# A chunked recurrent attention with a gated MLP on one core: filler matmuls, mask program, transfers and down-product waits changed together

## The chip, the core and the metric

One core of a Trainium2 chip runs the kernel as one program on five engines: TensorE (PE, with its weight loads PEld), VectorE (DVE), ScalarE (ACT), GpSimd (POOL) and SyncE (SP, which here only issues DMAs). The metric is the device time of one execution in microseconds; lower is better.

## The reference

The input x has 2048 rows of 640. After a layer norm, attention runs over 64 segments of 32 rows, one after the other: each segment is headed by 8 memory rows, which are the first 8 output rows of the segment before. 32 heads of 128, a causal mask, and the output product Wo. Then a gated MLP with 1728 hidden columns. Both have a residual.

```python
for s in range(n_seg):
    h = jnp.concatenate([mem, xs], axis=1)          # 8 + 32 rows
    q, k, v = h @ Wq, h @ Wk, h @ Wv                 # per head
    p = softmax(where(mask, q k^T * scale, -1e9))
    o = (p v) @ Wo
    mem = o[:, :M]
    outs.append(o[:, M:])
h = x + attention
h2 = h + (relu(gate) * up) @ W_down                  # gate, up: layernorm(h) @ W_gate, W_up
```

The segments form a serial chain; the MLP (rows in four blocks of 512) can only start on rows that are done.

## The kernel before, in words

The program is recorded as a list of operations, each with keys that it reads and writes (`add`, L38). `solve` (L45) turns the keys into semaphore waits; each engine then runs its own operations in the order in which they were recorded. So the order in the source is the order on each engine, and a wait holds up all that is queued behind it on the same engine. A key that names a finer part of a tile gives a wait for that part alone.

**Opening** (masks from L293, the rest L719 to L940). SP issues the 15 weight transfers of W (five row chunks of 1 MB each for K, Q and V), then 8 pieces of Wo (640 KB each, keys ("Wo", half, group)), then one input load. Meanwhile POOL builds constants, among them the two masks `mca` and `mbd` by chains of affine_select (L293 to L316). PE projects K, Q and V for the first segment and the first group of memory-side rows, in the order in which the W chunks land: K and Q chunk by chunk, then `first_values` (L766) for V, chunks 0 to 2, the scores of segment 0 (`scores`, L475), and V chunks 3 and 4. Then come the memory part of the softmax (`pv_mem`, L528), the products with the first half of Wo (`wo_pairs`, L591, four groups, each waits for its Wo piece), the second half (`wo_pass`, L574, four groups), and between them projections and `keep_busy` (L882): matmuls whose result in bank T1 nobody reads. keep_busy(n, cut) issues 4n products of 512 columns, each cut into `cut` matmuls. The segment's result goes through DVE (L614, L615) into act_r, from which segment 1 starts.

**Segments 1 to 63** (from L945). Each projects K, Q and V, does scores, softmax and products with V and Wo, and hands 8 rows on by `fold_split` (L600) and `to_act_split` (L612). `fold_split(bk, eng)` puts its addition (L606) on the engine that it is given. Values are also copied by DMA into VM (`merge_v`, L648), which `pv_x` (L663) reads in the next segment. Every fourth segment projects rows for the four segments to come from act_e (`extra_units`, L789). In segment 60 POOL copies rows into act_e (L1087).

**MLP.** W's space is reused once the projections are done. `load_piece(key)` (L780) takes the next piece of W_gate or W_up off a list (column groups 0 to 255, 256 to 511, 512 to 1023, and so on; from 512 on each group comes in two row halves) and issues it once `key` has been written. xn2T, the normed rows of block 0, is loaded in segment 62 (L996). `gate_up(b, j)` (L839) makes hidden columns 128j to 128j+127; the ones of block 0 begin amid segment 63. `load_down` (L1155) loads W_down in pieces of three row chunks, keys ("Wd", 0) to ("Wd", 6); `down_part` and `down_tails` (L1091, L1106) multiply with it.

In the trace, helpers appear under one line: L386 and L359 are projection matmuls (L359 reuses loaded weights, also in L1100's products), L410 the copies on ACT, L324 all DMA issues, L347 DMA transposes, L121 a wait of its own.

## Time and profile before

| | us |
|---|---|
| median of 3 runs | 1005.47 (1005.17 to 1006.03) |
| the profiled execution | 1004.47 |
| its span, first to last instruction | 1002.7 |
| PE busy | 970.9 (97%), 26,097 matmuls |
| PE weight loads | 537.8 (54%), 24,920 |
| DVE busy | 715.6 (71%) |
| ACT busy | 524.9 (52%) |
| POOL busy | 167.8 (17%) |
| mean granted TensorE clock | 0.997 |

The page's first part gives busy time by engine, the second the span in 40 slices, the fourth the chain of work that ended last: followed back from the last instruction, at each step to what released it. What lies on that chain sets the time; an engine that is idle beside it costs nothing. The span is divided into the opening (0 to 58 us), 63 segments of about 12 us (58 to 821 us), and the MLP, whose first products begin at 813 us. The list of waits adds up, for each line, how long its engine stood idle before it and what ended that. The timeline gives single instructions, and a query by windows the busy time, clock and DMA share of any stretch.

### The profile page before, as it was taken

How to read it: one execution, taken by the hardware profiler on the slowest of the kernel's cores; microseconds unless marked ns; L12 is line 12 of the kernel's file. 1: busy time of each engine (PE TensorE's matmuls, PEld its weight loads, DVE VectorE, ACT ScalarE, POOL GpSimd, SP SyncE). 2: the span in 40 equal slices, each digit the busy share in tenths (PEclk: the TensorE clock that was granted, in tenths of full speed). 3: DMA queues.
4: the chain of work that ended last, by engine and by line, in shares of the span. 5: the costliest groups of instructions: out<-in, count | busy, mean ns of one | idle time of the engine just before them, and what ended most of it. 6: DMA issues, size and time to landing. Idle time of an engine off the chain costs nothing.

```text
span 1002.7 us, 56369 instructions
## 1 busy us (share of the span) xinstructions
PE 970.9 (97%) x26097; PEld 537.8 (54%) x24920; DVE 715.6 (71%) x1863; ACT 524.9 (52%) x1330; POOL 167.8 (17%) x416
## 2 busy tenths in 40 slices
PE   3789999999999999999999999999999999999998
PEld 1255555556555555555556555655555554344443
DVE  2558787878888887888788878787878756345332
ACT  0456666666666666666666666566666643122121
POOL 7011202021302130222022212111110010000000
PEclk9899999999999999999999999999999999999999
DMA  9921212121222122111312131211121168413100
GB/s 374 417 96 36 53 29 53 28 56 55 54 41 54 48 54 46 48 54 47 53 41 63 48 55 40 41 41 39 40 40 34 44 175 242 103 20 93 27 14 26
DMA packets 73103, 73.34 MB, mean 73 GB/s; under 512 B 42304, under 2 KB 59680, under 8 KB 70944
## 3 DMA queue, kind: packets, MB, share of 16 engines
q1 hardware_dynamic: 70736, 68.44, 24.5%
q8 instruction: 200, 3.28, 1.4%
q10 hardware_dynamic: 2128, 1.31, 0.5%
q14 instruction: 39, 0.32, 0.1%
HBM read 37.04 MB, written 6.55 MB: 43 GB/s over the span
## 4 chain that ended last, share of the span: by engine, by line
PE 93%; DMA 3%; SPq 2%; DVE 1%; issue 1%; ACT 0%; POOL 0%; DVEq 0%; ACTq 0%
PE ps L386 47%; PE ps L850 10%; PE ps L359 7%; PE ps L574 7%; PE ps L591 7%; PE ps L634 4%; PE ps L1100 3%; DMA W<-in_A_Wv_dram 3%; PE ps L475 2%; PE ps L663 2%; PE ps L528 2%; SPq L324 1%; DMA Wd<-in_B_W_down_dram 0%; PE ps L889 0%; PE ps L863 0%
## 5 line engine op out<-in xcount | busy, mean ns | idle before, releaser
L386 PE MATMUL ps<-W,act_r 128*32 128x512 bf16 (+1 forms) x8369 | 454.4, 358 | 2.9 <-DVE act_r L615 1.8
L386 PEld LDWEIGHTS ps<-W,act_r 128*32 128x32 bf16 x8369 | 212.9, 96 | 168.3 <-DVE act_r L615 33.1
L410 ACT ACTIVATE tok<-ps 128x512 bf16<-128x512 f32 x190 | 109.4, 594 | 57.1 <-PE ps L386 48.7
L386 PE MATMUL ps<-W,act_e 128*32 128x512 bf16 x1224 | 120.8, 385 | 8.2 <-DMA W<-in_A_Wv_dram 4.2
L405 DVE STREAM_TRANSPOSE Ko<-tox 128x512 bf16<-128x512 bf16 x128 | 89.8, 702 | 38.9 <-ACT tox L410 36.6
L483 POOL COPY Qo<-Qe 128x256 bf16<-128x256 bf16 x64 | 28.0, 437 | 529.4 <-DVE oT L548 522.4
L410 ACT ACTIVATE tox<-ps 128x512 bf16<-128x512 f32 x134 | 79.6, 598 | 53.1 <-PE ps L386 32.0
L554 DVE STREAM_TRANSPOSE oT<-tox 128x512 bf16<-128x512 bf16 x128 | 94.2, 736 | 0.0
L405 DVE STREAM_TRANSPOSE Qo<-tok 128x512 bf16<-128x512 bf16 x124 | 85.5, 690 | 0.8
L359 PE MATMUL ps<-W,act_e 128*32 128x512 bf16 x856 | 85.5, 387 | 0.0
L574 PE MATMUL ps<-Wo,oT 128*32 128x160 bf16 x4032 | 82.4, 233 | 0.9 <-issue 0.9
L591 PE MATMUL ps<-Wo,oT 128*32 128x320 bf16 x2016 | 80.4, 300 | 0.0
L574 PEld LDWEIGHTS ps<-Wo,oT 128*32 128x32 bf16 x4032 | 71.4, 97 | 9.7 <-DVE oT L548 3.1
L410 ACT ACTIVATE Vp<-ps 128x512 bf16<-128x512 f32 x127 | 75.2, 592 | 0.7 <-ACT Vp L410 0.5
L878 ACT ACTIVATE g<-ps 128x512 bf16<-128x512 f32 x52 | 30.1, 593 | 80.1 <-PE ps L850 80.1
L604 ACT ACTIVATE SA<-TA 64x40 f32<-64x40 f32 x126 | 29.5, 234 | 75.8 <-DVE TA L602 75.0
L879 DVE TENSOR_TENSOR hT<-g,ps 128x512 bf16<-128x512 bf16 x52 | 35.7, 687 | 40.7 <-PE ps L850 38.7
L491 ACT ACTIVATE Pm<-ps 128x64 bf16<-128x64 f32 x126 | 28.2, 224 | 69.8 <-PE ps L475 69.7
L850 PE MATMUL ps<-xn2T,Wu 128*128 128x512 bf16 x259 | 64.5, 379 | 0.1
L850 PE MATMUL ps<-xn2T,Wg 128*128 128x512 bf16 x247 | 61.8, 379 | 1.3 <-issue 1.0
L591 PEld LDWEIGHTS ps<-Wo,oT 128*32 128x32 bf16 x2016 | 53.1, 97 | 15.3 <-DVE rm L538 0.9
L548 DVE STREAM_TRANSPOSE oT<-om 128x128 bf16<-128x128 bf16 x126 | 39.1, 310 | 31.1 <-ACT om L540 31.1
(113 smaller groups left out, 1441.0 us busy)
## 6 DMA issues: line engine op xcount, KB each, us to landing
VM<-Vp SPq DMA_DIRECT2D x126, 65.0 KB
VM<-Vp SPq DMA_DIRECT2D x63, 130.0 KB
W<-in_A_Wk_dram SPq DMA_DIRECT2D x5, 1024.0 KB
W<-in_A_Wq_dram SPq DMA_DIRECT2D x5, 1024.0 KB
W<-in_A_Wv_dram SPq DMA_DIRECT2D x5, 1024.0 KB
Wo<-in_A_Wo_dram SPq DMA_DIRECT2D x8, 640.0 KB
attn_d<-wtok SPq DMA_DIRECT2D x248, 7.5 KB
xt<-in_A_x_dram SPq DMA_DIRECT2D x16, 160.0 KB
```

The costliest lines, as they stand in the source:

```text
L359: return pe.add_instruction(mybir.InstMatmult(name=nc.get_next_instruction_name(), engine=mybir.EngineType.PE, ins=[pe.lower_ap(rhs), pe.l ...
L386: ins = pe.matmul(*b, start=(c == ends[0]), stop=(c == ends[1]), skip_group_check=True)
L405: add("dve", lambda v: v.transpose(dst[:, 16 * i:16 * i + 16, 0:32], tok[t][:, :].rearrange("p (h f) -> p h f", f=32)), r=tok_keys(t), w=keys)
L410: add("act", lambda a: a.activation(dst, src, ACTF.Copy), r=r, w=w)
L548: add("dve", lambda v: v.transpose(ap(oT[par], 160 * hf, [[40, 4], [320, 4], [1, 8]]), ap(om, 128 * hf, [[1, 4], [4, 32]])), r=[("om", hf) ...
L554: add("dve", lambda v, kh=kh: v.transpose(ap(oT[p], 160 * kh + M, [[320, 4], [40, 4], [1, 32]]), ap(tox, 128 * kh, [[256, 4], [1, 4], [4, ...
L574: i = pe.matmul(bank(bk)[32 * gg:32 * gg + 32, 0:160], src[:, hb, 0:32], w[:, gg], start=(hb == CH[16 * halves[0]]), stop=(hb == CH[-1]), ...
L591: i = pe.matmul(bank(bk)[32 * q:32 * q + 32, 0:320], src[:, hb, 0:32], w, start=(n == 0), stop=(n == 7), skip_group_check=True)
L634: ins = pe.matmul(bank(bk)[32 * q:32 * q + 32, 0:320], src[:, hb, 0:32], w[:, 2 * (q % 2):2 * (q % 2) + 2], start=(i == 0), stop=(i == 15) ...
L850: ins = pe.matmul(bank(bk), w[:, c, lo:lo + 128], xn2T[par][:, c, :], start=(c == 0), stop=(c == DC - 1))
L878: add("act", lambda a: a.activation(g1[gi][:, :], bank(bg), ACTF.Relu), r=[B(bg)], w=[("g1", gi)])
L879: add("dve", lambda v: v.tensor_tensor(hT[par][:, j, :], g1[gi][:, :], bank(bu), ALU.mult), r=[B(bu), ("g1", gi)], w=[("hT", par, j)])
```

## The change

It does these things:

- In the opening's mask program the four affine_selects of rows 0 to 31 that have the same pattern become one over four tiles.
- keep_busy takes a column count in place of the cut. The three fillers between the groups of L591 issue 16 matmuls of 512 columns each (they had 32 of 256, 32 of 256 and 64 of 128). A new filler of 80 matmuls of 32 columns stands between value chunks 3 and 4.
- xn2T is loaded by four transfers (row chunks 0, 1, 2, and 3 with 4) in place of one. All who read it still wait for all four.
- The fifth weight piece (W_gate, columns 512 to 1023, row chunks 0 to 2) is issued by SP instead of ACT, after the key ("VM", 0, 3), in the program behind the row stores of `rows(P3, ...)`.
- In segment 61 the addition of fold_split moves from DVE to POOL.
- POOL's copy into act_e in segment 60 also waits for the rows that to_act_split writes (L615).
- down_part and down_tails wait only for the pieces of W_down that they read.

```diff
@@ -295,7 +295,12 @@
         for j in range(4):
             for r in range(2):
                 sl, n = mca[32 * g:32 * g + 32, j, r, :], 0 if r == g % 2 else 1 + j
-                add("pool", lambda p, sl=sl, n=n: p.affine_select(sl, sl, [[1, SEG]], ALU.is_ge, 0.0,
+                pat = [[1, SEG]]
+                if g == 0 and n == 0:
+                    if j:
+                        continue
+                    sl, pat = mca[0:32, :, r, :], [[0, 4], [1, SEG]]
+                add("pool", lambda p, sl=sl, n=n, pat=pat: p.affine_select(sl, sl, pat, ALU.is_ge, 0.0,
                                                                   base=M if n == 0 else M * (n - 1) - RID,
                                                                   channel_multiplier=-1), r=[("mca",)], w=[("mca",)])
                 if n > 1:
@@ -879,21 +884,21 @@
         add("dve", lambda v: v.tensor_tensor(hT[par][:, j, :], g1[gi][:, :], bank(bu), ALU.mult),
             r=[B(bu), ("g1", gi)], w=[("hT", par, j)])
 
-    def keep_busy(n, cut=1):
-        wide = 512 // cut
+    def keep_busy(n, cols=512):
 
         def f(pe):
             for g in range(4 * n):
                 o = 32 * (g % 4)
-                for q in range(cut):
-                    i = pe.matmul(bank(T1)[o:o + 32, 0:wide], xe[:, 0, :], W[:, 2, 0, 0:wide], start=True, stop=True,
-                                  skip_group_check=True)
+                i = pe.matmul(bank(T1)[o:o + 32, 0:cols], xe[:, 0, :], W[:, 2, 0, 0:cols], start=True, stop=True,
+                              skip_group_check=True)
             return i
         add("pe", f, r=xke + [("W", 2, 0)], w=[B(T1)])
 
     scores(0, 0)
     scores(0, 1)
-    first_values(range(3, DC))
+    first_values((3,))
+    keep_busy(20, 32)
+    first_values((4,))
     for hf in range(2):
         exp_mem(0, hf)
         mask_mem(0, hf)
@@ -919,7 +924,7 @@
     for g in range(4):
         wo_pairs(0, T0, g)
         if g:
-            keep_busy(4, (1, 2, 2, 4)[g])
+            keep_busy(4)
     fold_split(T0, "pool")
     for g in range(3):
         wo_pass(0, P3, (1,), (g,))
@@ -993,8 +998,9 @@
                 norm_x_late(0)
                 flip_ox(s - 1, (0,))
             if s == NSEG - 2:
-                dma(xn2T[0][:, :, :], xn2_d[:, :, :], r=[("xn2_d", u) for u in range(4)] + [("Wdone", 0)],
-                    w=[("xn2", 0, u) for u in range(4)])
+                for n, (lo, hi) in enumerate(((0, 1), (1, 2), (2, 3), (3, DC))):
+                    dma(xn2T[0][:, lo:hi, :], xn2_d[:, lo:hi, :], r=[("xn2_d", u) for u in range(4)] + [("Wdone", 0)],
+                        w=[("xn2", 0, n)])
             project(a, ks, 2, (0,), (P2,), range(4), held=not last and held[2])
             scores(s, 0, (0, 1))
             project(a, ks, 2, (0,), (P2,), (4,))
@@ -1018,7 +1024,6 @@
             gate_up(0, 0)
             scores(s, 1)
             exp_x(s, 1)
-            load_piece(("g1", 0), "act")
             mask_x(s)
             late_o(s - 1)
             break
@@ -1063,7 +1068,7 @@
             dma(xt[:, :], x_ap[128 * e2:128 * e2 + 128, :], w=[("xt",)])
             load_attn(at, e2, [], ("at",))
         wo_split(par, P1)
-        fold_split(P1, "dve" if s % 4 == 1 else "pool")
+        fold_split(P1, "dve" if s % 4 == 1 and s != NSEG - 3 else "pool")
         wo_pass(par, P3, (1,))
         to_act_split(s + 1, P3)
         if s >= 1:
@@ -1085,7 +1090,7 @@
         if s == NSEG - 4:
             p, j = place(NSEG - 1)
             add("pool", lambda o, p=p, j=j: o.tensor_copy(act_e[1 - p][:, :, M:32], act_r[p][:, j, :, M:32]),
-                r=[("act", p, "x", j), ("act", p, "x")], w=[("acte", 1 - p)])
+                r=[("act", p, "x", j), ("act", p, "x"), ("act", *place(s + 1), "m")], w=[("acte", 1 - p)])
 
 
     def down_part(par, u, bks, js, hfs=(0, 1)):
@@ -1101,7 +1106,8 @@
                     else:
                         i = again(pe, *a, j == 0, j == FC - 1, None)
             return i
-        add("pe", f, r=[("hT", par, j) for j in js] + [("Wd", n) for n in range(7)], w=[B(bks[hf]) for hf in hfs])
+        wk = sorted({n for j in js for n in ((j // 3,) if j < FC - 1 else (5, 6))})
+        add("pe", f, r=[("hT", par, j) for j in js] + [("Wd", n) for n in wk], w=[B(bks[hf]) for hf in hfs])
 
     def down_tails(par, u0, bks):
 
@@ -1113,7 +1119,7 @@
                                   Wd[p0:p0 + FR, FC - 1, hf * 320:(hf + 1) * 320], start=False, stop=True,
                                   skip_group_check=True)
             return i
-        add("pe", f, r=[("hT", par, FC - 1)] + [("Wd", n) for n in range(7)], w=[B(bk) for q in range(2) for bk in bks[q]])
+        add("pe", f, r=[("hT", par, FC - 1), ("Wd", 5), ("Wd", 6)], w=[B(bk) for q in range(2) for bk in bks[q]])
 
     def down_out(par, u, bks, o, hfs=(0, 1)):
         for hf in hfs:
@@ -1178,6 +1184,7 @@
 
     rows(P3, s % 2, s - 1)
     gate_up(0, 1)
+    load_piece(("VM", 0, 3))
     load_piece(("hT", 0, 0))
     pv_x(s, P0)
     norm_x(P0)
```

## Prediction

> **What bounds the kernel now.** I read the page's chain of work first, then the list of what TensorE (PE) waited for, then the two places where that list is not empty: the opening (0 to 58 us) and the hand-over to the second half (800 to 852 us).

> ```profile
> PE 93%; DMA 3%; SPq 2%; DVE 1%; issue 1%; ACT 0%; POOL 0%; DVEq 0%; ACTq 0%
> ```

> PE sets the end. Only time in which PE stands still on the chain, or runs at less than full clock, can be gained. PE's waits, from the list of waits filtered to PE (line, releaser, total us, times, longest):

> ```profile
> PE ps L386 <- DMA W<-in_A_Wv_dram: 4.2, 4, 1.4
> ...
> PE ps L889 <- issue: 1.5, 1, 1.5
> ...
> PE ps L850 <- issue: 1.0, 6, 0.2
> ...
> PE ps L574 <- issue: 0.9, 1, 0.9
> ...
> PE ps L1100 <- DMA Wd<-in_B_W_down_dram: 0.5, 1, 0.5
> PE ps L663 <- issue: 0.4, 1, 0.4
> ```

> "issue" means that no semaphore explains the wait. The change touches five of these. The other thing to see is the clock. Three stretches of 3.41 us of the opening (time, length, PE, PEld, DVE, ACT, POOL busy, clock, DMA share, GB/s):

> ```profile
> 38.95:42.36 3.41, 1.36 (x52) 0.41 (x33) 0.63 (x4) 1.00 (x4) 0.00 (x0) 1.00 1.00 410
> 42.36:45.77 3.41, 2.30 (x33) 0.71 (x28) 1.71 (x3) 1.20 (x2) 0.00 (x0) 0.50 1.02 411
> 45.77:49.18 3.41, 3.41 (x54) 1.69 (x41) 2.81 (x9) 2.35 (x3) 0.44 (x1) 0.50 1.02 413
> ```

> After a stretch with PE busy 1.36 us of 3.41 the clock halves at 42.36; it comes back at 49.18, after a stretch with no gap. All that time the DMA engines are full (1.02). The PE timeline of that time (start, length):

> ```profile
> 42.69 0.62 PE L386 MATMUL ps<-W,act_e 128*32 128x512 bf16 x4 [1.43 <-DMA W<-in_A_Wv_dram]
> ...
> 51.14 0.83 PE L889 MATMUL ps<-W,act_e 128*32 128x128 bf16 x39
> 53.47 0.47 PE L889 MATMUL ps<-W,act_e 128*32 128x128 bf16 x19 [1.50 <-issue]
> ...
> 56.51 0.51 PE L574 MATMUL ps<-Wo,oT 128*32 128x160 bf16 x12
> ...
> 58.33 0.40 PE L386 MATMUL ps<-W,act_r 128*32 128x512 bf16 x4 [0.52 <-DVE act_r L615]
> ```

> PE stops for 1.5 us in the middle of 64 filler matmuls, where no wait stands. I take this for PE's own instruction supply: the page's instruction queue q8 moved 200 packets, 3.28 MB, for 51,017 PE instructions, so one packet carries 256. Counting instructions (a matmul that loads weights is two, a wait of its own one), this stall and the 0.9 us one at 805.2 stand at the same place modulo 256. In windows of 0.1 us the packets before them show at 51.0 and 803.7; PE went on 2.4 us later both times (53.47, 806.13).

> **The opening.** (1) A filler of 80 matmuls of 32 columns goes between value chunks 3 and 4. Its cost alone: the 64 score matmuls of 40 columns at L475 start within 38.59 to 39.05, 0.031 us per four, so 20 fours take 0.6 us, in the 1.4 us wait before 42.69. It would be free. But by the count the 256-boundary before the one in the stall lies after its 48th matmul. The packet for that block shows at 41.4 in the trace, and the program ahead of its request is unchanged; with the 2.4 us above the block is there at 43.9. So PE stops in the filler until 43.9, the other 32 matmuls take 0.25 us, and value chunk 4 starts at 44.2 instead of 42.69: 1.5 us late. PE gains some 0.4 us of busy time before 42.36 (1.36 to about 1.75); I assume that the clock still halves.

> (2) The three later fillers have 16 matmuls each, where they had 32, 32 and 64; their columns are the same, so their time is (16 x 512 columns, four at once, 0.216 us per four as at L386: 0.87 us each). The boundary now falls before the last of them, asked for at 43.9 and, by the opening's delay (request near 47.5, supply at 53.47: 6 us), there by 49.9. The 1.5 us stall goes.

> (3) The new schedule, at the old clock: chunk 4 to the first L591 took 42.69 to 47.46, so 44.2 + 4.8 = 49.0; two L591 groups at almost full clock 0.6; three fillers 2.6 and two L591 groups 0.54 make 52.75; the four L574 groups follow 0.92 us apart as before (53.74 to 56.51), the last at 55.5. **What is late next:** the last of the Wo pieces. The last W packet of 8 KB shows at 41.9 and PE used it at 42.69, 0.8 later; the last packet of Wo (between 2 and 8 KB) shows at 54.7, so it can be used at 55.5. Both limits agree: the last L574 group moves from 56.51 to 55.5, 1.0 us. With a full clock PE would only wait for Wo. From there to 58.33 the chain (L614, L615, L386) is unchanged, except that the next 256-boundary lies in the last filler; requested near 51, supplied at 56.5 to 57.5 while PE wants it at 55.9 and goes on at 57.3 anyway: 0 to 0.3 lost, I take 0.15. **Opening: -0.85.** Its ends: -1.0, and 0 if Wo is later still.

> [...]

> (4) Pool: four affine_selects become one. At 0.27 us from start to start, three less is 0.8 us; Pool's mask work ends at 27.1 and is first used at 39.4. Nothing.

> **Segments 60 and 61.** Deferring the Pool copy: in segment 60 it runs at 782.40 beside DVE's L615, which takes 0.29 us instead of 0.20 (segments 58, 59); PE's next L386 comes 0.78 after L614 starts instead of 0.69. **-0.09.** Segment 61's sum goes from DVE to Pool: L574 to the next L386 is 2.11 us there and 2.02 in 58 and 59, which use Pool. **-0.09.** Pool has nothing else then.

> **The load of xn2T in four.** SP issues four transfers (0.4 to 0.6 us each) instead of one of 0.58 at 800.05; the Wg load behind goes from 801.50 to about 802, the VM transfers wait for ACT until 803.27 anyway. PE needs xn2T at 813.44: hidden. What it can change is the 0.92 us stall at 805.2, as the packet at 803.7 shares the DMA engines with this load. Asked for near 801.8, it shows 1.9 us later; in the quiet stretch after 53.47 it is 1.3 (54.8), in the full opening over 3. So between -0.6 and +1.4; the bytes stay the same and the load here is between the two: **0.**

> **The weight load behind the last value transfers.** Wg columns 512 to 1023, rows of chunks 0 to 2 (384 KB) were sent from ACT at 816.03, right into the VM transfers that SP issued at 815.07 to 816.9; DMA share is 0.8 to 1.0 until 819. PE waits 0.42 us for VM at 820.33. Now it is issued on SP once VM has landed and behind the two row stores (819.14 to 819.84). VM is free of it; some 0.16 us stay, as with L850 at 813.44, which has as many waits and nothing late. **-0.26**, ends -0.42 and 0. Behind it on SP every issue is 0.4 later, first the other half of that Wg group, then xt and at. These are first wanted at 830.2 (gate_up 4) and 835.1 (L695). The 384 KB are 1.3 us at 300 GB/s, and of the 10 us from 820 the DMA engines are idle 21%: covered; without the cover up to 1.3 would show at 830. ACT's 0.37 us trigger stood before an idle 1.7 us.

> **Down products.** The first one waits 0.54 us for the last Wd piece. It now wants pieces 0 to 3 only; piece 3 was issued at 843.77, the last at 846.79 and landed at 851.2, so piece 3 is there some 3 us before PE ends L863 (850.67). A switch of 0.14 stays: **-0.40**, ends -0.54 and 0. The next wait is for piece 4, 24 matmuls of 0.136 us later. Behind it PE has no gap until the end, so the gain stays.

> **Sum:** -0.85 - 0.09 - 0.09 + 0 - 0.26 - 0.40 = -1.69. The profiled execution took 1004.47 us (span 1002.7 and 1.8 around it): 1002.8. The three timed runs have a median of 1005.47, 1.0 above it, so I give 1005.47 - 1.69 = **1003.8**, 0.17% less.

> **Rivals.** (A) *The fetch at 805 improves as well.* Smaller packets let the instruction packet through sooner: -0.6 more, and the ends of VM and Wd, -0.3: 1002.9. For it: the fetch is 0.6 slower there than in a quiet stretch. Against: same bytes, more packets. (B) *The opening gives nothing*: Wo's last piece lands at 56.5, because one more instruction packet shares the engines before 55, or the unprofiled runs lose less clock there: 1005.47 - 0.84 = 1004.6. (C) *Slower: the clock stays low.* It came back after a stretch that was busy 3.41 of 3.41 us and not after one with 2.30. In the new order the stretch 45.77 to 49.18 has a hole of 0.75 us while chunk 4 is evacuated, 2.65 busy. If that is not enough, everything from 49.18 to 52.6 runs at half: fillers of 1.72 instead of 0.87, the last L574 group at 58.05 instead of 56.51, +1.55; with -0.84 from the rest 1005.47 + 0.7 = 1006.2. It decides from where between 68% and 100% the clock returns. A second such stretch makes it 58.9: 1007.0. Against it: the 32 matmuls and chunk 4 may keep the clock up at 42.36 altogether. (D) *The filler isn't held up and the clock stays full*: Wo still bounds, same time as the forecast.

> **How the numbers follow.** Forecast with D 0.50, A 0.25, B 0.13, C 0.12. The range reaches from A with the spread of the runs (0.5 lower) to the fetch's bad end and part of C: 1002.4 to 1005.8. A measurement here can tell about 0.2%, 2.0 us. Faster by more: most of A and a part of the forecast's spread, 0.35. Slower by more: C's second stretch, or the fetch's bad end with C, 0.07. Within 0.2%: 0.58.

> **What would show it.** Right: the first value chunk after the filler starts near 44.2 with an "issue" gap inside L892; no gap before L579; last L579 group at 55.5; no L1105 wait on Wd; L668 gap 0.16. Wrong: chunk 4 at 42.7 (my block count is off), a clock of 0.5 after 49.2 (C), an "issue" gap near 804 much shorter or longer than 0.9, a wait at gate_up 4.

## The result, and the profile after

The changed kernel takes 1001.47 us (median, 1000.89 to 1001.98), the kernel before, run beside it, 1005.28 us (1004.13 to 1006.03): a ratio of 0.9963, 95% interval 0.9952 to 0.9974, or 3.8 us less. The forecast was 1003.8 with a range of 1002.4 to 1005.8: the time lies below the range. The profiled execution took 1001.56 us, its span 999.7, 3.0 less than the span before.

The chain of work that ended last, by engine, in the changed kernel:

```profile
PE 93%; SPq 3%; DMA 2%; DVE 1%; issue 0%; ACT 0%; DVEq 0%; ACTq 0%
```

TensorE (PE) still sets the end; "issue" has fallen from 1% to 0%. From PE's list of waits in the changed kernel (line, releaser, total us, times, longest):

```profile
PE ps L892 <- issue: 1.4, 1, 1.4
PE ps L579 <- DMA Wo<-in_A_Wo_dram: 0.9, 2, 0.5
...
PE ps L391 <- DVE act_r L620: 0.8, 1, 0.8
```

The waits on W_down, in front of the last pv_x and in L579 ("issue") are no longer in the list. A line of the list of before that the prediction did not take up has shrunk as well, from five waits to the one above (L620 here is L615 there):

```profile
PE ps L386 <- DVE act_r L615: 1.8, 5, 0.8
```

Of the four waits that are gone from the list one stood at the start of segment 1, the other three, 0.16 to 0.17 us each, in segments 11, 27 and 43; experiments 9 to 11 are about these. PE in the opening of the changed kernel (start, length):

```profile
41.80 0.52 PE L892 MATMUL ps<-W,act_e 128*32 128x32 bf16 x48
43.78 0.37 PE L892 MATMUL ps<-W,act_e 128*32 128x32 bf16 x32 [1.45 <-issue]
43.98 0.42 PE L391 MATMUL ps<-W,act_e 128*32 128x512 bf16 x4
...
53.96 0.46 PE L579 MATMUL ps<-Wo,oT 128*32 128x160 bf16 x16 [0.47 <-DMA Wo<-in_A_Wo_dram]
...
55.53 0.46 PE L579 MATMUL ps<-Wo,oT 128*32 128x160 bf16 x16 [0.47 <-DMA Wo<-in_A_Wo_dram]
...
57.19 0.62 PE L391 MATMUL ps<-W,act_r 128*32 128x512 bf16 x10
```

As forecast, PE stops after exactly 48 of the 80 new filler products, chunk 4 follows at 43.98 (forecast 44.2), and the last L579 group stands at 55.53 (55.5), held by the last Wo piece. Segment 1 begins at 57.19, 1.14 earlier.

The clock differs from the forecast. Stretches of 3.41 us, cut where the clock changes (columns as in the prediction):

```profile
34.69:38.10 3.41, 1.24 (x20) 0.31 (x12) 1.23 (x3) 0.00 (x0) 0.00 (x0) 1.00 1.01 420
38.10:41.51 3.41, 3.21 (x92) 1.24 (x76) 0.63 (x4) 1.00 (x4) 0.00 (x0) 0.50 1.01 416
41.51:44.92 3.41, 1.96 (x104) 1.00 (x88) 0.27 (x1) 0.27 (x1) 0.00 (x0) 1.00 1.00 404
```

It was low in one stretch, not two, and 4 us earlier than in the profile of before.

At 803 the stall of 0.92 us is gone: L579's 64 products run through, and segment 62 is 0.96 us shorter. But the first pv_x of segment 63 now takes 0.70 us where it took 0.48. Before:

```profile
806.13 1.15 PE L574 MATMUL ps<-Wo,oT 128*32 128x160 bf16 x56 [0.92 <-issue]
...
810.32 0.48 PE L663 MATMUL ps<-VM,Px 64*32 64x129 bf16 x32
```

In the changed kernel:

```profile
803.54 1.29 PE L579 MATMUL ps<-Wo,oT 128*32 128x160 bf16 x64
...
808.02 0.70 PE L668 MATMUL ps<-VM,Px 64*32 64x129 bf16 x32
```

One pair of profiles is a poor guide here. From the pv_x of segment 1 to that of segment 60 the two take the same, 712.30 and 712.28 us, and yet, as the experiments show, 0.87 us had been gained there and 0.87 lost again in this one execution: in intervals that are 12.08 to 12.12 us long otherwise, five of the changed kernel's (from the pv_x of segments 13, 21, 33, 41, 49) are 0.12 to 0.24 longer. All five are pauses in the middle of L579. Counted over PE's instructions they stand at the same place of a block (256 instructions: 51,017 over q8's 200 packets are 255 each) as the stall of 0.92 us: at number 194, modulo 256. Four segments have 3072 PE instructions, twelve blocks, so the place comes round in every fourth segment. Kernels with either opening show pauses at this place in some executions (0.22 us at 647.18 in kernel 1, with the new one, 0.25 at 456.29 in kernel 8, with the old) and not in others. So what follows compares means over all profiles with the same code in a stretch.

### The profile page after: what moved, and what is told of

Its sections match the earlier page's. It is cut to its first block, busy times and chain, and to the rows that moved or that the text cites. A ratio compares the mean times of both kernels' runs of the same rounds, so it can differ in the third digit from the quotient of the medians.

```text
span 999.7 us, 56383 instructions
## 1 busy us (share of the span) xinstructions
PE 971.8 (97%) x26111; PEld 539.2 (54%) x24920; DVE 715.3 (72%) x1862; ACT 524.4 (52%) x1330; POOL 167.6 (17%) x414
## 3 DMA queue, kind: packets, MB, share of 16 engines
q8 instruction: 200, 3.28, 1.4%
## 4 chain that ended last, share of the span: by engine, by line
PE 93%; SPq 3%; DMA 2%; DVE 1%; issue 0%; ACT 0%; DVEq 0%; ACTq 0%
PE ps L391 47%; PE ps L855 11%; PE ps L579 7%; PE ps L364 7%; PE ps L596 7%; PE ps L639 4%; SPq L329 3%; PE ps L1105 3%; PE ps L480 2%; PE ps L668 2%; DMA Wo<-in_A_Wo_dram 2%; PE ps L533 2%; PE ps L868 0%; PE ps L1118 0%; DVE oT L559 0%
## 5 line engine op out<-in xcount | busy, mean ns | idle before, releaser
L391 PEld LDWEIGHTS ps<-W,act_r 128*32 128x32 bf16 x8369 | 215.4, 96 | 163.5 <-DVE act_r L620 30.8
L415 ACT ACTIVATE tok<-ps 128x512 bf16<-128x512 f32 x190 | 109.3, 594 | 57.3 <-PE ps L391 48.8
L415 ACT ACTIVATE tox<-ps 128x512 bf16<-128x512 f32 x134 | 79.6, 598 | 52.3 <-PE ps L391 31.5
L579 PE MATMUL ps<-Wo,oT 128*32 128x160 bf16 x4032 | 82.6, 233 | 1.0 <-DMA Wo<-in_A_Wo_dram 0.9
L579 PEld LDWEIGHTS ps<-Wo,oT 128*32 128x32 bf16 x4032 | 70.6, 97 | 11.9 <-DVE oT L553 3.1
L855 PE MATMUL ps<-xn2T,Wg 128*128 128x512 bf16 x260 | 64.7, 379 | 0.0
```

The lines of the kernel that those rows point to most:

```text
L391: ins = pe.matmul(*b, start=(c == ends[0]), stop=(c == ends[1]), skip_group_check=True)
L415: add("act", lambda a: a.activation(dst, src, ACTF.Copy), r=r, w=w)
L579: i = pe.matmul(bank(bk)[32 * gg:32 * gg + 32, 0:160], src[:, hb, 0:32], w[:, gg], start=(hb == CH[16 * halves[0]]), stop=(hb == CH[-1]), ...
L855: ins = pe.matmul(bank(bk), w[:, c, lo:lo + 128], xn2T[par][:, c, :], start=(c == 0), stop=(c == DC - 1))
```

## The experiments

Ratios are to the kernel before, run beside it on the same chip, with 95% intervals. Intervals between segments are measured from one pv_x (L663, in kernels with five more lines L668) to the next; "segment 11" is the interval from the pv_x that segment 11 issues.

**1. The opening alone** (mask edit, new filler, uncut fillers; the rest as before).

```diff
+                if g == 0 and n == 0:
...
-    first_values(range(3, DC))
+    first_values((3,))
+    keep_busy(20, 32)
+    first_values((4,))
...
-            keep_busy(4, (1, 2, 2, 4)[g])
+            keep_busy(4)
```

> The kernel before with the opening's edits alone (mask program, the filler of 80 products between value chunks 3 and 4, three uncut fillers). Theory 1 (the last Wo piece is what is late next): the first product of segment 1 starts near 57.2 us instead of 58.33, and the median falls by 1.0 to 1.3 us; nothing else moves, the 0.9 us stall at 805 stays, only 1.1 us earlier. Theory 2 (the profile of after was one with a lucky clock phase): segment 1 starts between 57.2 and 58.3 and the clock is low somewhere between 42 and 50 us. On record the term was -0.85.

Measured: 1003.04 against 1004.73, ratio 0.9980 (0.9971 to 0.9989). Segment 1 starts at 57.65, after a last L579 group at 56.01 that waited 0.43 us for Wo, though the clock was low from 46.3 to 49.8. The stall near 804 is there (1.21 us). Theory 1 holds for the place; the time fell by more than the opening can give. The surplus was found in the intervals: segments 11, 27 and 43 took 12.05, 12.04 and 12.05 us, and 12.34, 12.32 and 12.33 in the kernel before. Nothing in my forecast says so.

**2. The same, with the filler elsewhere.**

```diff
-    first_values((3,))
-    keep_busy(20, 32)
-    first_values((4,))
+    first_values(range(3, DC))
...
         keep_busy(1)
+    keep_busy(20, 32)
```

> As the opening's edits alone, but the 80 filler products stand behind the third group of L579, in a wait for Wo, so value chunks 3 and 4 follow each other as before and the instruction count up to segment 1 is unchanged. The instruction block that stalled PE for 1.5 us at 53.5 now begins in the third L579 group, which waits for its Wo piece until about 54 anyway. Theory 1 (what counts is that no block boundary lies in the fillers; Wo bounds): no issue gap of over 0.3 us before 57 us, segment 1 starts at 57.2, median 1.0 to 1.3 below the kernel before, same as the opening's edits alone. Theory 3 (the filler earns by keeping the TensorE clock up): the clock is 0.5 over two stretches of 3.4 us between 38 and 50 us, and segment 1 starts at 58 or later, 0 to 0.3 us gained.

Measured: 1003.09, ratio 0.9983 (0.9974 to 0.9992), as the opening alone. Segment 1 starts at 57.72, with three waits for Wo and no stall over 0.31 us in the fillers. So the filler need not stand between the chunks; it has to move the block boundary out of the three fillers. Theory 3 could not be tried against it, for in this execution the clock never fell; but in kernels 7 and 12 below, which have the filler between the chunks, it fell at 43 all the same, so the filler did not hold it up there.

**3 and 4. xn2T in four transfers**, by row chunks (packets of 1 KB) and by partitions (5 KB, as in the single one).

```diff
-                dma(xn2T[0][:, :, :], xn2_d[:, :, :], r=[("xn2_d", u) for u in range(4)] + [("Wdone", 0)],
-                    w=[("xn2", 0, u) for u in range(4)])
+                for n, (lo, hi) in enumerate(((0, 1), (1, 2), (2, 3), (3, DC))):
+                    dma(xn2T[0][:, lo:hi, :], xn2_d[:, lo:hi, :], r=[("xn2_d", u) for u in range(4)] + [("Wdone", 0)],
+                        w=[("xn2", 0, n)])
```

and, for the partitions,

```diff
+                for n in range(4):
+                    o = 32 * n
+                    dma(xn2T[0][o:o + 32, :, :], xn2_d[o:o + 32, :, :], r=[("xn2_d", u) for u in range(4)] + [("Wdone", 0)],
+                        w=[("xn2", 0, n)])
```

> The kernel before with xn2T loaded by four transfers, one for each row chunk (packets of 1 KB), and nothing else. On record this was 0. Theory 4 (it is what lets the instruction packet through): the issue gap of 0.92 us before L574 near 805 is gone and the median falls by 0.9 to 1.0 us. Rival (the gap went in the changed kernel because PE came there 1.6 us earlier relative to the loads): the gap stays at 0.6 to 1.2 us, and the time is the same within 0.3 us.

> The kernel before with xn2T loaded by four transfers that each take 32 partitions (rows of 5 KB, as in the one transfer), and nothing else. If the size of the packets is what matters, the issue gap of 0.92 us near 805 stays. If four issues matter, which spread the load over 3 us of SP and send the weight load behind it 1 us later, the gap goes and 0.9 us are gained as with four row chunks.

Measured: 1003.70, ratio 0.9993 (0.9982 to 1.0003), and 1005.40, ratio 1.0002 (0.9993 to 1.0011). By their intervals neither time is told from no change; the traces decide. The stall is gone in both, so the size of the packets is not the reason. DMA queues in windows of 0.2 us, first before (803.6 to 803.8), then 3 (801.4 to 801.6), then 4 (804.7 to 804.9); q8, with 200 packets for 51,017 PE instructions, I take to carry these:

```profile
DMA packets 63, 0.05 MB, mean 243 GB/s; under 512 B 8, under 2 KB 61, under 8 KB 62
...
q8 instruction: 1, 0.02, 27.8%
```

```profile
DMA packets 68, 0.08 MB, mean 384 GB/s; under 512 B 8, under 2 KB 67, under 8 KB 67
...
q8 instruction: 1, 0.02, 31.4%
...
xn2T<-xn_d SPq DMA_DIRECT2D x1, 256.0 KB
```

```profile
DMA packets 23, 0.08 MB, mean 389 GB/s; under 512 B 10, under 2 KB 10, under 8 KB 22
...
q8 instruction: 1, 0.02, 36.3%
```

In before the instruction packet appears when the single transfer, which runs at 415 GB/s from 802.4 to 803.4, has drained: of the 63 packets of its window 61 are under 2 KB and one is the instruction block, so that at most one is left of xn2T's 5 KB. In 3 and 4 it appears amid the pieces; in 3 the last piece is only being issued. That four transfers by partitions gave no time has two reasons in its trace, which is of the slowest of its eleven executions (1006.16 us): PE waits for the values' transfers, which now stand behind the four (0.25 us ahead of segment 63's first pv_x, 0.53 ahead of its last), and the clock was low from 37.5 to 44.4 and from 54.6 to 58.0, so that segment 1 started at 60.10.

```profile
PE ps L663 <- DMA VM<-Vp: 0.8, 2, 0.5
```

**5. The weight piece alone.**

```diff
-            load_piece(("g1", 0), "act")
...
+    load_piece(("VM", 0, 3))
```

> The kernel before with the fifth weight piece alone moved from ACT to SP behind the last value transfers. On record: -0.26 (-0.42 to 0). Theory: the 0.42 us in front of the last segment's pv_x (L663 near 820) goes entirely, and nothing waits at gate_up 4, so segment 63's pv_x to the first Down product is 0.4 us shorter; the rest as before (the 0.9 us at 805 stays). Rival: with the piece on SP the later pieces come later and PE waits up to 1.3 us near 830. The median alone can't show 0.4 us; it is read from the trace. Where segment 1 starts (57.4 to 60) adds to how the same opening code scatters.

Measured: 1004.32, ratio 0.9993 (0.9984 to 1.0002): not told from nothing by its time. In the trace segment 63 takes 9.93 us, before 10.42; PE has no wait near 830. Over seven profiles with the old order it varies from 9.87 to 10.52, mean 10.23, and two of them (6 and 9) lose nothing; with the piece moved and no other stall it is 9.87 to 9.93 in three.

**6. The Down products' waits alone.**

```diff
-        add("pe", f, r=[("hT", par, j) for j in js] + [("Wd", n) for n in range(7)], w=[B(bks[hf]) for hf in hfs])
+        wk = sorted({n for j in js for n in ((j // 3,) if j < FC - 1 else (5, 6))})
+        add("pe", f, r=[("hT", par, j) for j in js] + [("Wd", n) for n in wk], w=[B(bks[hf]) for hf in hfs])
...
-        add("pe", f, r=[("hT", par, FC - 1)] + [("Wd", n) for n in range(7)], w=[B(bk) for q in range(2) for bk in bks[q]])
+        add("pe", f, r=[("hT", par, FC - 1), ("Wd", 5), ("Wd", 6)], w=[B(bk) for q in range(2) for bk in bks[q]])
```

> The kernel before with the Down products' waits alone cut to the pieces that they read. On record: -0.40 (-0.54 to 0). Theory: the wait at L1100 (0.54 us in before, 0.3 in one run, none in two others with before's waits) is never there; gain between 0 and 0.7 us by how late the last piece happens to land, and no new wait at the products that read pieces 4 to 6. Rival: the wait only moves to piece 4 or 5, a few products later, and the gain is under 0.2.

Measured: 1005.21, ratio 0.9996 (0.9987 to 1.0005). From L863 to the first Down product it takes 1.09 us, as in the changed kernel, and no later product waits. With the old keys ten profiles have 1.15 to 1.80, mean 1.43.

**7. The changed kernel with one xn2T transfer.**

```diff
-                for n, (lo, hi) in enumerate(((0, 1), (1, 2), (2, 3), (3, DC))):
-                    dma(xn2T[0][:, lo:hi, :], xn2_d[:, lo:hi, :], r=[("xn2_d", u) for u in range(4)] + [("Wdone", 0)],
+                dma(xn2T[0][:, :, :], xn2_d[:, :, :], r=[("xn2_d", u) for u in range(4)] + [("Wdone", 0)],
...
```

> The changed kernel with xn2T in one transfer again. Theory 4 (the four issues keep the instruction packet from standing behind 640 KB): the issue gap of 0.9 to 1.2 us before L579 near 803 is back, its packet shows 1.9 us or more after it is asked for, and the median is 0.9 to 1.2 above the changed kernel's. Rival (the gap was a matter of when PE came there): no gap, same time as the changed kernel.

Measured: 1002.13, ratio 0.9960 (0.9947 to 0.9974). The stall is back, the longest of all, and segment 62 takes 13.63 us (12.17 in the changed kernel):

```profile
805.19 1.15 PE L579 MATMUL ps<-Wo,oT 128*32 128x160 bf16 x56 [1.42 <-issue]
```

The ratio cannot tell this from the changed kernel's 0.9963: the expected 0.9 to 1.2 us are inside the intervals. In the profiles 1.5 us lost in segment 62 stand against gains elsewhere: L668 runs in 0.42 us here, the five pauses of the changed kernel's profile are nearly absent (one of 0.10), and the end of the program, after PE's last product, is 0.19 us shorter (see the table below).

**8. One transfer, issued later** (the kernel before, the transfer moved behind the values' transfers).

```diff
-            if s == NSEG - 2:
-                dma(xn2T[0][:, :, :], xn2_d[:, :, :], r=[("xn2_d", u) for u in range(4)] + [("Wdone", 0)],
...
         merge_v(s, 0)
+        if s == NSEG - 2:
+            dma(xn2T[0][:, :, :], xn2_d[:, :, :], r=[("xn2_d", u) for u in range(4)] + [("Wdone", 0)],
...
```

> The kernel before with the single xn2T transfer of 640 KB moved in SP's order from ahead of the fourth weight piece's predecessor to behind the values' transfers (near 804 instead of 800). Theory 4 as a rule of order (the instruction packet waits for what was handed to the queue shortly ahead of its request at 801.8, whatever its packets' size): the gap at 805 goes with one transfer too, about -0.9, and the packet of the next block, asked for at about 804.3, now stands behind the 640 KB and is late at L663, 808.9: a gap of 0 to 1 us there. Rival (one large transfer holds up a request at any place near it): the gap at 805 stays.

Measured: 1003.16, ratio 0.9982 (0.9973 to 0.9990). SP's queue, and segment 62 takes 12.18 us:

```profile
803.11 0.42 SPq L324 DMA_DIRECT2D Wg<-in_B_W_gate_dram  x1
804.84 1.80 SPq L324 DMA_DIRECT2D VM<-Vp  x3
806.68 0.59 SPq L324 DMA_DIRECT2D xn2T<-xn_d  x1
```

The stall is gone with a single transfer, L663 runs in 0.42 with no gap, and segment 63 takes 9.87 without the moved weight piece. So it is the order: issued at 800.05, ahead of the block's packet (803.7), the 640 KB came with a stall of 0.92 us in before; issued at 806.68, behind it (803.4 to 803.6), with none. The expected cost at the next block did not come.

**9, 10 and 11. What shortens segments 11, 27 and 43:** the mask edit alone; the filler edits alone; and the kernel before with two more instructions on POOL, whose edit this is (the other two are parts of the diff above):

```diff
-                if n > 1:
+                for _ in range((n > 1) * (3 if (g, j) == (3, 3) else 1)):
...
```

> The kernel before with the mask edit alone (four affine_selects of POOL become one). On record this was nothing. Theory 5: POOL's program gets three instructions shorter, and the places where POOL crosses from one block of its instructions to the next, 128 apart, no longer fall on the addition L606 on the critical chain; segments 11, 27 and 43 take 12.04 us instead of 12.33, -0.87 in all. Rival (the short segments belong to the fillers or to the order of the opening): the three segments stay at 12.33, nothing gained.

> The kernel before with the opening's filler edits alone, without the mask edit. Theory 1 and 5: segment 1 starts near 57.2 to 57.7 us (57.4 to 60.1 with the old fillers), segments 11, 27 and 43 stay at 12.33; median 0.8 to 1.2 below the kernel before. Rival: the three segments are at 12.04 here.

> The kernel before with two more instructions on POOL in the opening: the last affine_select of the mask is done three times over, which changes no value. Theory 5 (the place of the block's boundary): POOL's addition in these segments stands at the same distance from the boundary as in the changed kernel (128 is 5 times 25 and 3; three less and two more differ by the five instructions of a segment), so segments 11, 27 and 43 take 12.04 with more work on POOL, -0.87. Rival (less work on POOL in the opening is what helps): 12.33, and no gain.

Measured: 1003.11, ratio 0.9986 (0.9977 to 0.9995); 1003.80, ratio 0.9988 (0.9979 to 0.9998); 1004.35, ratio 0.9987 (0.9979 to 0.9996).

| segment | before | 9 mask | 10 fillers | 11 two more | after |
|---|---|---|---|---|---|
| 11 | 12.34 | 12.04 | 12.33 | 12.04 | 12.03 |
| 27 | 12.32 | 12.05 | 12.33 | 12.04 | 12.04 |
| 43 | 12.33 | 12.05 | 12.33 | 12.05 | 12.04 |

Less work on POOL and more work on POOL give the same 0.29 us three times; so it is the number of its instructions that matters, not the work. POOL, DVE and PE at the end of segment 11, before:

```profile
189.63 0.40 POOL L563 COPY oTe<-oT 128x256 bf16<-128x256 bf16 x1
190.78 0.27 POOL L606 TENSOR_TENSOR SA<-SA,TA 128x40 f32<-128x40 f32 x1 [0.76 <-DVE TBf L614]
```

```profile
191.16 0.20 DVE L615 TENSOR_TENSOR act_r<-TBf,SA 128x40 bf16<-128x40 f32 x1 [0.37 <-POOL SA L606]
```

```profile
191.41 2.35 PE L386 MATMUL ps<-W,act_r 128*32 128x512 bf16 x50 [0.17 <-DVE act_r L615]
```

and POOL in kernel 11:

```profile
188.91 0.40 POOL L563 COPY oTe<-oT 128x256 bf16<-128x256 bf16 x1
189.77 0.27 POOL L606 TENSOR_TENSOR SA<-SA,TA 128x40 f32<-128x40 f32 x1 [0.46 <-ACT SA L604]
```

In before the addition starts 0.75 us after the copy ended, in kernel 11 0.46. The releaser that the trace names in before (TBf, begun on DVE at 190.43) is not an operand of L606; it only came last. Counted from the start of POOL's program, and from 0, L606 is instruction 196, 324 and 452 in these segments of before: 128 apart, and in no other segment at that place of 128. With three instructions less or two more (a segment has five) the instruction at 196 is the copy L563 instead, which follows 0.4 us of POOL's own work and starts no later. The packets of q14, the other instruction queue, move with it: one shows at 191.43 us in before, 0.65 after L606 started, at 189.61 in kernel 11 and at 201.22 in the changed kernel, 0.70 and 0.73 after the copy at 196 started (in segments 27 and 43 of before 1.7 and 1.9 after L606). From these places I take it that a block of POOL's program begins there; what the 0.29 us are spent on at its start no view shows. From L606 the delay runs through L615 to PE with no slack.

**12. A version from the findings:** the changed kernel with one xn2T transfer behind the values' transfers (the edit of 8).

```diff
-            if s == NSEG - 2:
-                for n, (lo, hi) in enumerate(((0, 1), (1, 2), (2, 3), (3, DC))):
-                    dma(xn2T[0][:, lo:hi, :], xn2_d[:, lo:hi, :], r=[("xn2_d", u) for u in range(4)] + [("Wdone", 0)],
...
         merge_v(s, 0)
+        if s == NSEG - 2:
+            dma(xn2T[0][:, :, :], xn2_d[:, :, :], r=[("xn2_d", u) for u in range(4)] + [("Wdone", 0)],
...
```

> The changed kernel with xn2T in one transfer again, issued behind the value transfers of segment 62, as in the run that moved it in the kernel before. Expected: no gap of over 0.3 us before L579 near 803, no stall of 0.28 inside L668 at 808 (the weight load there comes later), segments 62 and 63 12.1 and 9.9 us long instead of 12.17 and 10.16: 0 to 0.4 below the changed kernel, about 1001.3. Rival: the next block of instructions is held up in L668 by the single transfer, 0.3 to 1 more.

Measured: 1001.16, ratio 0.9961 (0.9948 to 0.9973). Segments 62 and 63 take 12.17 and 9.88, and nothing is lost in L668:

```profile
803.94 1.29 PE L579 MATMUL ps<-Wo,oT 128*32 128x160 bf16 x64
808.41 0.42 PE L668 MATMUL ps<-VM,Px 64*32 64x129 bf16 x32
```

By the trace it is 0.28 us better than the changed kernel there, and 0.19 at the end of the program; by its time, 0.31 below, the two cannot be told apart.

## Why the prediction was wrong, step by step

Means over the profiles with the same code in that stretch (ends in brackets):

| step | old code | new code | measured | on record |
|---|---|---|---|---|
| start of segment 1 | 58.52 (57.41 to 60.10, 8) | 57.44 (57.03 to 57.69, 5) | -1.08 | -0.85 |
| POOL's mask program: segments 11, 27, 43 | 12.33 each (7) | 12.04 each (7) | -0.87 | nothing |
| segments 60 and 61 together | 24.27 (11) | 24.10 (3) | -0.17 | -0.18 |
| xn2T: segment 62 | 13.29 (12.83 to 13.63, 9) | 12.17 (3 and after) | -1.12 | 0 |
| weight piece: segment 63 | 10.23 (9.87 to 10.52, 7) | 9.89 (9.87 to 9.93, 3) | -0.34 | -0.26 |
| new pause in L668 (after only) | 0 | 0.28 | +0.28 | not seen |
| L863 to the first Down product | 1.43 (1.15 to 1.80, 10) | 1.09 (4) | -0.34 | -0.40 |
| PE's last product to the end | 2.97 (11) | 3.15 (3, 4 and after) | +0.18 | not seen |

Kernel 2, with its filler elsewhere, is not in the first row; its segment 1 starts at 57.72. The sum is -3.5; the medians differ by 3.8, and the interval of the ratio reaches from 2.6 to 4.8 us. The forecast had -1.69.

The last row is a cost of the four transfers that neither the forecast nor the experiments looked for. At the end SP goes through 24 waits, some 0.06 us apart, one of which lasts until 2.16 to 2.17 us after PE's last product in every profile, 0.4 after the last DMA packet; I take it for the wait on the last output. It is the 18th in the eleven kernels with one xn2T transfer and the 15th in 3, 4 and the changed kernel, so that three more waits follow it there.

Two terms taken at zero failed, and they make up most of the miss.

**"(4) Pool: four affine_selects become one ... Nothing." It measured -0.87.** I priced the instructions (0.8 us in a span where POOL waits) and they are indeed free. I had counted PE's instructions for block boundaries and did not count POOL's, although POOL's addition L606 is on the chain in three segments of four. The 12.33 of segments 11, 27 and 43 stands in the profile of before, 16 segments apart, with three waits on act_r in the list of PE's waits, and I did not look for it. Shown by 9, 10 and 11.

**"The load of xn2T in four ... 0." It measured -1.12, the larger of the two.** I named the mechanism and bounded it at -0.6 to +1.4, with "the bytes stay the same". The bytes did not decide. In before the single transfer was issued by 800.6 and ran at 415 GB/s, with the DMA engines full (1.00), from 802.4 to 803.4, and the block's packet showed at 803.7, behind it; four were issued over 2.0 to 3.2 us of SP, and the packet showed among their pieces. When a block is asked for no view shows: the times of request on record (43.9, 47.5 and 51 in the opening, 801.8 here) were my estimates. What shows is the packet: the next one came 1.3 us after PE went on at 53.47 in before (54.8), and 3.8 us after it went on at 43.78 in the changed kernel (47.55). My lower end, -0.6, took the 1.3 us of a quiet stretch as the best fetch and left 0.3 of the stall; in fact none was left, and the stall of 0.92 was below its mean: it lasts 0.60 to 1.42 us in the nine profiles that have it, 1.08 on average. Rival A named this stage, but by "smaller packets", which 4 and 8 refute.

**The opening, -0.85.** The chain of reasons held (48 products, the stop in the filler, chunk 4 at 44, Wo late next at 55.5), apart from the clock, which I assumed to be halved from 42.36. The start of segment 1 that follows from the forecast, 58.33 less 0.85, is 57.48, and the new opening's mean is 57.44; what is off is the old opening, whose size was taken from one execution. That opening is a lottery: its stall in the fillers lasts from 1.35 to 2.45 us, and the TensorE clock falls in different stretches, once during the stall itself (kernel 6, low from 52.3 to 55.8) so that segment 1 began at 58.92 although the stall had ended earlier than in before. The new opening varies by 0.7 us only. In three of its five profiles (1, 10, after) the last L579 group waits for Wo; in 7 and 12, where the clock was low from 43 on, it comes at 56.0 without a wait. Rival C, a loss by a low clock, was not seen there: the low clock from 43.1 to 49.9 in kernel 7 left segment 1 at 57.66. The clock beside PE's busy time stands at the end of this document: it stayed full after stretches with PE busy 1.44 us or more of 3.41, so that by those rows the 1.75 us estimated for the new filler would have kept it up, and C's 2.65 lies just between the stretches after which it stayed low (up to 2.57) and those after which it came back (from 2.69).

**The weight piece and the Down products** were right in their mechanism, both within the ends given. The 0.16 us that I left in front of pv_x do not stay (in the changed kernel nothing is listed there), nor do the 0.14 in front of the Down products. The 0.16 were a misreading. The row that they were taken from has four products where the program has five (`gate_up` goes over five row chunks); before, then after:

```profile
813.44 1.03 PE L850 MATMUL ps<-xn2T,Wg 128*128 128x512 bf16 x4 [0.16 <-issue]
```

```profile
811.13 1.25 PE L855 MATMUL ps<-xn2T,Wg 128*128 128x512 bf16 x5
```

One record is missing in the profile of before, and the gap is its place. Nine of the fourteen profiles lack such records and five do not, and in all of them L863 starts 28.67 us after the last pv_x. **Segments 60 and 61** were right. **B** and **D**: the opening gave its gain, and the filler was held up.

**The starting time.** 1005.47 was a fair median (1004.73 to 1005.28 beside the other kernels). The time fell out of the range for the two terms above, 2.0 us together, which were taken at zero.

What stays open: what the 0.29 us at the start of a POOL block are; why the pauses of 0.1 to 0.4 us in L579 come in some executions only, and whether the block's packet in L668 at 808 was late by the weight load whose packets of 512 bytes move from 804.0 to 805.2, right behind which it shows (805.29). Kernel 12 fits that (there they move from 802.0 to 803.5, and the packet shows at 805.15), but it was not tried by itself.

## What to carry to other kernels

Three instructions less on POOL, or two more, took three segments from 12.33 to 12.04 us, and the edits of PE's fillers took the stall of 1.35 to 2.45 us out of the three between the groups. So where an edit changes the number of instructions on an engine that stands on the critical chain, count what that does to the later ones, even if the work itself is hidden, and look in the segment times for a loss that returns at a fixed distance (here 16 segments). Before a large transfer is issued, ask which other packets will stand behind it, and try putting it after them: here that did with one transfer what cutting it in four did (segment 62 at 12.18 and 12.17 us, 13.29 before), without the longer end (2.97 us, not 3.15). Where a stage scatters between executions, as the old opening did (segment 1 from 57.41 to 60.10), one profile doesn't price it: collect the same stretch from all the profiles that share its code.
